# Weights' sign by a parametric ReLU, high parts of w_out on VectorE, and the second tile turned by VectorE and DMA

## The chip, the cores and the metric

One NeuronCore of a Trainium2 chip. The metric is device time in microseconds, the median of several executions. TensorE (PE) multiplies, VectorE (DVE) and ScalarE (ACT) work element by element, GpSimd (POOL) does little here, and SyncE (SP) issues nearly all DMAs. Each engine takes its own list of instructions in order, and semaphores between the lists make one engine wait for another.

## The reference

Chunked attention (chunks of 64 tokens, 8 heads of 64) and behind it a feed-forward block with a piecewise quadratic activation. All inputs arrive in double precision.

```python
scores = scale * np.matmul(q_c, k_c.transpose(0, 1, 2, 4, 3))
attn = np.exp(scores - np.max(scores, axis=-1, keepdims=True))
attn = attn / (np.sum(attn, axis=-1, keepdims=True) + 1e-09)
out = np.matmul(attn, v_c)
...
h = x @ w_in
g = np.where(h >= 1, h, np.where(h <= -1, 0.0, (h + 1) ** 2 / 4))
return g @ w_out
```

There are 4608 tokens; x has 512 columns, w_in is 512 x 2048, w_out 2048 x 512.

## The kernel before

**Tiles.** The 4608 tokens are nine tiles t of 512 tokens. A tile has four groups g of two heads; group (t, g) is worked on as one [128, 512] piece. The feed-forward block has 16 steps j of 128 hidden columns: `ffn_in(t, j)` is twelve 512-column products (four chunks kc of x, each with three products of high and low parts), and `ffn_out(t, j - 2)`, two steps behind, is twelve more. `ffn_in` needs the split x of all four groups: chunk kc comes from group kc. So tile 1 of the feed-forward block can't go past its first three chunks until group (1, 3) of the attention is done.

**Attention of a group.** `attn_turn` turns q and k so that heads lie along partitions; `scores_of` multiplies (L420); `attn_softmax` takes the maximum (L474), on tile 1 eight exponentials that also sum (L483), the reciprocal and the scaling of e (L506); `attn_turn_back` turns e into aT; `values_of` multiplies aT with v (L441); `attn_split` writes the high part xh (ACT, L545) and the low part xl (DVE, L546). From the second tile on, the values of one group and the scores of the next stand together on PE (`attn_products`), and both use the bank pair `ps_a`. There is one buffer for each of qT, kT and x (in the attention's sense: the turned e), and two for e, aT and v.

**Two ways to turn.** Tiles below `FLIPPED` (here tiles 0 and 1) turn q, k and e by four PE transposes each (`flip`, L376) into a PSUM bank, which ACT evicts (L401, L529). Later tiles load q and k in blocks of 32 (`load_blocks`, 128-byte rows, four DMAs each), turn them by a DVE 32 x 32 stream transpose (L392), and turn e by a DVE transpose (L533) and eight DMAs on SP that put the blocks into place (`move`, L522).

**Weights.** All 32 weight chunks, 512 KB of doubles each, are loaded once (L249, L256) and made into a high and a low single-precision part by `prepare(w, j)` while tile 0 computes. A double is read as two 32-bit words. ACT scales the upper word, read as a float (L271); DVE shifts it left by three (L274); ACT scales the lower word (L277); DVE adds it (L281) and puts the sign bit in (L286); ACT rounds to the high part (L296); DVE subtracts for the low part (L300). Each step j of tile 0 prepares two chunks.

**The order.** Nothing is scheduled at run time. The kernel records each piece of work with an engine, a cost and what it reads and writes; `Plan.emit` then plays this through with its own clock and emits the instructions of each engine in the order of that play: of the pieces that are ready on a free engine, the one recorded first. A DMA's landing is put behind all DMAs planned before it:

```python
if moving:
    end = moved = max(end, moved) + moving
for m in users[n]:
    other = parts[m][0]
    delay = lag + (0.0 if other == e == "pe" else self.DELAY[e])
    ready[m] = max(ready[m], end + delay)
```

A weight load has `moving` 1.9, a blocked q or k load 2.2, the eight DMAs of `move` 0.4 and a cost of 4.8 on SP. So a changed cost, or another way to turn, moves pieces on every engine. At the start, where PE has nothing to do, dummy products (`warm`, L734) fill in.

Of the kernel before, what the change touches and what calls it, by code (L numbers as in the profile page):

```python
# [9 lines left out]
F32 = mybir.dt.float32  # L10
F32R = mybir.dt.float32r
AF = mybir.ActivationFunctionType
ALU = mybir.AluOpType
# [4 lines left out]
class Plan:  # L18
# [15 lines left out]
    def add(  # L34
        self, engine, cost, emit, reads=(), writes=(), lag=0.0, columns=0, port=False, moving=0.0
    ):
        n = len(self.parts)
        needs = {self.writer[k] for k in (*reads, *writes) if k in self.writer}
        for k in writes:
            needs.update(self.readers.pop(k, ()))  # L40
            self.writer[k] = n
        for k in reads:
            self.readers.setdefault(k, []).append(n)
        needs.discard(n)
        for k in writes:
            self.written.setdefault(k, []).append(n)
        self.parts.append((engine, cost, emit, needs, lag, columns, port, moving))
        return n
# [92 lines left out]
def kernel(  # L141
# [15 lines left out]
    nc = tc.nc  # L157
# [16 lines left out]
    SCALE = 1.0 / float(D) ** 0.5  # L174
    ALL = NTILE * NP

    FLIPPED = 2
    EARLY = 2

    BATCH = (0, 1, 2, 3, None, 4, 5, 6, 7)  # L180
# [35 lines left out]
    weight = {}  # L216

    def place(kind, w, j, shape, dtype):
        return sb.tile(shape, dtype, name=f"{kind}_{w}{j}", tag=f"{w}{j}")

    first = {}
    for w, j, names in (
# [5 lines left out]
        both = place("first", w, j, [P, 2, T], F32)  # L228
# [3 lines left out]
    def room(name, bufs, t, g):  # L232
        if t == 0 and (name, g) in first:
            return first[name, g]
        return bufs[(t * NP + g) % len(bufs)]

    plan = Plan()
    count = {"tmp": 0}

    def turn_of(name, bufs):  # L240
        count[name] += 1
        return bufs[count[name] % len(bufs)]
# [17 lines left out]
    def prepare(w, j):  # L260

        both = (f"{w}{j}_0", f"{w}{j}_1")
        ykey, yf = turn_of("tmp", tmp_bufs)
        y = yf.bitcast(U32)

        def half(n):
            return words[w, j].rearrange("p (n two) -> p n two", two=2)[:, :, n]

        plan.add("act", 0.52, lambda: nc.scalar.activation(  # L271
            out=yf, in_=half(1).bitcast(F32), func=AF.Copy, scale=2.0 ** -112
        ), both, (ykey,))
        plan.add("dve", 0.34, lambda: nc.vector.tensor_scalar(  # L274
            out=y, in0=y, scalar1=3, scalar2=None, op0=ALU.logical_shift_left
        ), (), (ykey,), port=True)
        plan.add("act", 0.52, lambda: nc.scalar.activation(  # L277
            out=half(0), in_=half(0), func=AF.Copy, scale=2.0 ** -29
        ), (), both)

        plan.add("dve", 0.6, lambda: nc.vector.tensor_tensor(  # L281
            out=y, in0=y, in1=half(0), op=ALU.add
        ), both, (ykey,), port=True)

        def sign():
            nc.vector.scalar_tensor_tensor(  # L286
                out=y, in0=half(1), scalar=0x80000000, in1=y,
                op0=ALU.bitwise_and, op1=ALU.bitwise_or,
            )
            words.pop((w, j))  # L290

        plan.add("dve", 0.6, sign, both, (ykey,), port=True)

        def high():
            weight[w, j] = place("parts", w, j, [P, 2, T], F32R)
            nc.scalar.copy(out=weight[w, j][:, 0, :], in_=yf)  # L296

        def low():
            hi, lo = (weight[w, j][:, n, :] for n in range(2))
            nc.vector.tensor_tensor(out=lo, in0=yf, in1=hi.bitcast(F32), op=ALU.subtract)  # L300

        plan.add("act", 0.52, high, (ykey,), both)
        plan.add("dve", 0.6, low, (ykey, both[0]), (both[1],), port=True)


# [50 lines left out]
    def load_heads(t, g, which="qkv"):  # L356
        for n, src, bufs in (("q", q, q_bufs), ("k", k, k_bufs), ("v", v, v_bufs)):
            if n not in which:
                continue
            key, dst = room(n, bufs, t, g)  # L360
            load = load_values if n == "v" else load_rows if t < FLIPPED else load_blocks
            parts = 4 if load == load_blocks else 2
# [22 lines left out]
    def attn_turn(t, g):  # L385
        for n, (name, bufs, src_bufs, dst_bufs) in enumerate(
# [3 lines left out]
            dkey, dst = room(bufs, dst_bufs, t, g)  # L390
            if t >= FLIPPED:
                plan.add("dve", 0.6, lambda src=src, dst=dst: nc.vector.transpose(  # L392
# [34 lines left out]
    def values_of(t, g):  # L427
# [6 lines left out]
        def emit():  # L434
            for n in range(CT // 2):
                for h in range(2):
                    at = (2 * n + h) * C if t < FLIPPED else h * HALF + n * C
                    of = h * HALF + n * C
# [24 lines left out]
    def attn_softmax(t, g):  # L463
# [4 lines left out]
        e3 = e.rearrange("p (n k) -> p n k", k=C)  # L468
        e4 = e.rearrange("p (n h k) -> p h n k" if t < FLIPPED else "p (h n k) -> p h n k", h=2, k=C)
        mx4 = mx.rearrange("p (h n) x -> p h n x", h=2)  # L470
        sm4 = sm.rearrange("p (n h) x -> p h n x" if t < FLIPPED else "p (h n) x -> p h n x", h=2)
        sc = pair[:, :, :HALF].rearrange("p h (n k) -> p h n k", k=C)
# [37 lines left out]
    def attn_turn_back(t, g):  # L510
# [14 lines left out]

        if t < FLIPPED:
            pkey, ps = o_banks[1] if t == 0 else a_banks[0]
# [148 lines left out]
    load_more(6)  # L676
    load_heads(1, 1)
    prepare("wi", 0)
    prepare("wi", 1)
    prepare("wi", 2)  # L680

    LAG = 2
# [91 lines left out]
```

## Time and profile before

| | |
|---|---|
| timed runs | 865.99, 866.38, 867.03 us; median 866.38 |
| span of the profiled execution | 864.3 us, 14919 instructions |
| PE | busy 858.2 us (99%) |
| DVE, ACT | busy 443.8 us (51%), 382.6 us (44%) |
| DMA | 62.86 MB, mean 73 GB/s; 235920 of 250965 packets under 512 B |

The page gives the span of one profiled execution; of that execution's own time beyond the span it shows nothing, so the timed runs stand beside it. Durations of one row can overlap with the next on the same engine; where that matters, the distance between starts is used. A row of the timeline reads: start, length (us), engine, line, operation, output<-input, shapes, count. TensorE's granted clock is 1.00 in all windows of the profile.

### The profile page before, as it was taken

Reading aid. Unit: us, or ns where it says so; the run is one execution under the profiler, and the core shown is the slowest. Engines: PE = TensorE matmul, PEld = TensorE weight load, DVE = VectorE, ACT = ScalarE, POOL = GpSimd, SP = SyncE. Lnnn points to the kernel's source line nnn. Section 1 sums busy time; section 2 is a strip of 40 time slices with the busy share of each in tenths; the row PEclk is TensorE's granted clock in tenths of the full one; section 3 lists DMA queues with packets and bytes.
Section 4 is the critical chain, followed back from the end, with each engine's and each line's share of the span. In section 5 each row is a group of like instructions: output and inputs, shape, how many; then the busy total and the mean of one; then the engine's idle time right before and its main releaser. Section 6 shows DMA issues by size and latency. Waiting matters only on the chain.

```text
span 864.3 us, 14919 instructions
## 1 busy us (share of the span) xinstructions
PE 858.2 (99%) x5958; PEld 706.7 (82%) x5958; DVE 443.8 (51%) x762; ACT 382.6 (44%) x704; POOL 4.9 (1%) x10
## 2 busy tenths in 40 slices
PE   9999999999999999999999999999999999999998
PEld 8788788888888888888888888888888888888886
DVE  5999986444544444444544454445444444423222
ACT  5999965333433343333333343334333333333332
POOL 1000000000000000000000000000000000000000
PEclk9999999999999999999999999999999999999999
DMA  9997235322322232223322242223222310001001
GB/s 209 324 350 190 38 69 121 58 50 47 82 46 47 44 88 52 51 38 57 90 50 50 50 95 52 47 46 94 48 39 46 79 33 14 13 1 50 1 0 49
DMA packets 250965, 62.86 MB, mean 73 GB/s; under 512 B 235920, under 2 KB 244368, under 8 KB 250896
## 3 DMA queue, kind: packets, MB, share of 16 engines
q1 hardware_dynamic: 248640, 61.25, 31.7%
q8 instruction: 47, 0.77, 0.4%
q10 hardware_dynamic: 2256, 0.66, 0.4%
q14 instruction: 22, 0.18, 0.1%
HBM read 45.09 MB, written 9.44 MB: 63 GB/s over the span
## 4 chain that ended last, share of the span: by engine, by line
PE 91%; ACT 5%; DVE 2%; issue 1%; DMA 0%; POOL 0%; DVEq 0%; POOLq 0%; ACTq 0%
PE ps_h L562 42%; PE ps_o L597 41%; PE ps_a L441 2%; PE ps_a L420 2%; PE ps_h L734 1%; PE ps_a L597 1%; ACT tmp L271 1%; PE ps_o L376 1%; ACT r L572 1%; ACT words_wi L277 1%; ACT r L569 1%; ACT e L483 1%; ACT parts_wi L296 0%; DVE tmp L281 0%; ACT words_wo L277 0%
## 5 line engine op out<-in xcount | busy, mean ns | idle before, releaser
L562 PE MATMUL ps_h<-xh,parts_wi 128*128 128x512 f32 x1144 | 382.0, 393 | 0.0
L597 PE MATMUL ps_o<-parts_wo,gh 128*128 128x512 f32 x1120 | 346.1, 390 | 0.6 <-DVE parts_wo L300 0.4
L562 PEld LDWEIGHTS ps_h<-xh,parts_wi 128*128 128x128 f32 x1144 | 214.7, 188 | 46.2 <-DVE r L573 0.2
L597 PEld LDWEIGHTS ps_o<-parts_wo,gh 128*128 128x128 f32 x1120 | 209.6, 188 | 44.8 <-DVE parts_wo L300 0.7
L573 DVE SCALAR_TENSOR_TENSOR r<-ps_h,r 128x512 f32<-128x512 f32 x143 | 97.3, 681 | 259.1 <-ACT r L572 259.0
L562 PE MATMUL ps_h<-xl,parts_wi 128*128 128x512 f32 x572 | 222.9, 390 | 0.0
L597 PE MATMUL ps_o<-parts_wo,gl 128*128 128x512 f32 x560 | 218.0, 389 | 0.4 <-DVE gl L583 0.4
L569 ACT ACTIVATE r<-ps_h 128x512 f32<-128x512 f32 x143 | 86.1, 602 | 279.0 <-PE ps_h L562 279.0
L582 ACT CAST gh<-r 128x512 fp32r<-128x512 f32 x144 | 90.3, 627 | 147.8 <-PE ps_o L597 96.3
L583 DVE TENSOR_TENSOR gl<-r,gh 128x512 fp32r<-128x512 f32 x144 | 98.3, 682 | 107.1 <-ACT gh L582 106.9
L562 PEld LDWEIGHTS ps_h<-xl,parts_wi 128*128 128x128 f32 x572 | 107.4, 188 | 21.2
L597 PEld LDWEIGHTS ps_o<-parts_wo,gl 128*128 128x128 f32 x560 | 105.1, 188 | 22.7 <-DVE gl L583 0.8
L572 ACT ACTIVATE r<-r 128x512 f32<-128x512 f32 x144 | 91.6, 636 | 3.3
L474 DVE TENSOR_REDUCE mx<-ps_a 128x8 f32<-128x512 f32 x34 | 23.4, 688 | 27.0 <-ACT xh L545 18.0
L545 ACT CAST xh<-ps_a 128x512 fp32r<-128x512 f32 x34 | 20.0, 588 | 19.7 <-PE ps_a L420 19.2
L441 PEld LDWEIGHTS ps_a<-aT,v_sb 64*64 64x64 f32 x1056 | 18.4, 134 | 11.5 <-issue 10.8
L499 DVE TENSOR_REDUCE sm<-e 128x8 f32<-128x512 f32 x30 | 20.5, 685 | 10.7 <-ACT e L493 10.6
L441 PE MATMUL ps_a<-aT,v_sb 64*64 64x64 f32 x1056 | 22.9, 224 | 0.0
L546 DVE TENSOR_TENSOR xl<-ps_a,xh 128x512 fp32r<-128x512 f32 x34 | 22.4, 658 | 0.2 <-ACT xh L545 0.2
L506 DVE TENSOR_TENSOR e<-e,sm 128x512 f32<-128x512 f32 x32 | 21.8, 682 | 0.0
L420 PE MATMUL ps_a<-kT,qT 64*64 64x64 f32 x1056 | 21.4, 218 | 0.0
L533 DVE STREAM_TRANSPOSE x<-e 128x512 f32<-128x512 f32 x28 | 19.9, 711 | 0.9
(95 smaller groups left out, 422.8 us busy)
## 6 DMA issues: line engine op xcount, KB each, us to landing
words_wi<-in_moe_w_in_dram SPq DMA_DIRECT2D x16, 512.0 KB, 7.0
words_wo<-in_moe_w_out_dram SPq DMA_DIRECT2D x16, 512.0 KB, 7.1
out_dram<-tmp SPq DMA_DIRECT2D x31, 256.0 KB, 2.5
v_sb<-in_v_dram SPq DMA_DIRECT2D x60, 128.0 KB, 3.0
aT<-x SPq DMA_DIRECT2D x224, 32.0 KB, 1.9
q_sb<-in_q_dram SPq DMA_DIRECT2D x96, 64.0 KB, 2.2
k_sb<-in_k_dram SPq DMA_DIRECT2D x96, 64.0 KB, 2.3
q_sb<-in_q_dram SPq DMA_DIRECT2D x12, 128.0 KB, 6.6
```

The source lines that it names most:

```text
L420: nc.tensor.matmul(out=pair[i * C:(i + 1) * C, half, n * C:(n + 1) * C], lhsT=qT[rows, at], rhs=kT[rows, at], start=True, stop=True,)
L441: nc.tensor.matmul(out=pair[h * C:(h + 1) * C, half, HALF + n * C:HALF + (n + 1) * C], lhsT=v_sb[rows, of:of + C], rhs=aT[rows, at:at + C] ...
L474: plan.add("dve", 0.6, lambda: nc.vector.tensor_reduce(out=mx4, in_=sc, axis=AX.X, op=ALU.max), pkeys, (mkey,))
L506: plan.add("pool" if on_pool else "dve", 1.05 if on_pool else 0.6, lambda: eng.tensor_tensor(out=e3, in0=e3, in1=sm.broadcast_to([P, G, C] ...
L546: plan.add("dve", 0.6, lambda: nc.vector.tensor_tensor(out=of_tokens(xl), in0=ps, in1=of_tokens(xh.bitcast(F32)), op=ALU.subtract), (*pkey ...
L562: nc.tensor.matmul(out=ps, lhsT=weight["wi", j][:, half, kc * P:(kc + 1) * P], rhs=x, start=(kc == 0 and i == 0), stop=(kc == KC - 1 and i ...
L569: plan.add("act", 0.48, lambda: nc.scalar.activation(out=r, in_=ps, func=AF.Relu, bias=0.5, scale=0.5), (pkey,), (rkey,))
L572: plan.add("act", 0.52, lambda: nc.scalar.square(out=r, in_=r), (), (rkey,))
L573: plan.add("dve", 0.6, lambda: nc.vector.scalar_tensor_tensor(out=r, in0=ps, scalar=1.0, in1=r, op0=ALU.max, op1=ALU.min), (pkey,), (rkey,))
L582: plan.add("act", 0.52, lambda: nc.scalar.copy(out=gh, in_=r), (rkey,), (ghkey,))
L583: plan.add("dve", 0.6, lambda: nc.vector.tensor_tensor(out=gl, in0=r, in1=gh.bitcast(F32), op=ALU.subtract), (rkey, ghkey), (glkey,), port ...
L597: nc.tensor.matmul(out=acc, lhsT=x[:, cols], rhs=weight["wo", j][:, half, :], start=(j == 0 and i == 0), stop=(j == NF - 1 and i == 2),)
```

## The change

Three things. The sign of a weight is no longer put in by DVE: ACT scales the upper word with a parametric ReLU whose slope for negative inputs is 2^32, which adds 32 to the exponent of a negative number, so that the shift by three moves that bit to the sign's place. The high part of a w_out chunk is copied by DVE, that of a w_in chunk by ACT as before. And `FLIPPED` goes from 2 to 1, so tile 1 is loaded and turned as the later tiles are. Some costs of the plan change as well.

```diff
-    FLIPPED = 2
+    FLIPPED = 1
...
-        plan.add("act", 0.52, lambda: nc.scalar.activation(
-            out=yf, in_=half(1).bitcast(F32), func=AF.Copy, scale=2.0 ** -112
+        plan.add("act", 0.56, lambda: nc.scalar.activation(
+            out=yf, in_=half(1).bitcast(F32), func=AF.Prelu, scale=2.0 ** -112, alpha=2.0 ** 32
         ), both, (ykey,))
-        plan.add("dve", 0.34, lambda: nc.vector.tensor_scalar(
+        plan.add("dve", 0.38, lambda: nc.vector.tensor_scalar(
             out=y, in0=y, scalar1=3, scalar2=None, op0=ALU.logical_shift_left
         ), (), (ykey,), port=True)
-        plan.add("act", 0.52, lambda: nc.scalar.activation(
+        plan.add("act", 0.56, lambda: nc.scalar.activation(
             out=half(0), in_=half(0), func=AF.Copy, scale=2.0 ** -29
         ), (), both)
-        plan.add("dve", 0.6, lambda: nc.vector.tensor_tensor(
-            out=y, in0=y, in1=half(0), op=ALU.add
-        ), both, (ykey,), port=True)
-
-        def sign():
-            nc.vector.scalar_tensor_tensor(
-                out=y, in0=half(1), scalar=0x80000000, in1=y,
-                op0=ALU.bitwise_and, op1=ALU.bitwise_or,
-            )
+        def add():
+            nc.vector.tensor_tensor(out=y, in0=y, in1=half(0), op=ALU.add)
             words.pop((w, j))
-        plan.add("dve", 0.6, sign, both, (ykey,), port=True)
+        plan.add("dve", 0.6, add, both, (ykey,), port=True)
         def high():
             weight[w, j] = place("parts", w, j, [P, 2, T], F32R)
-            nc.scalar.copy(out=weight[w, j][:, 0, :], in_=yf)
+            hi = weight[w, j][:, 0, :]
+            if w == "wo":
+                nc.vector.tensor_copy(out=hi, in_=yf)
+            else:
+                nc.scalar.copy(out=hi, in_=yf)
...
-        plan.add("act", 0.52, high, (ykey,), both)
+        if w == "wo":
+            plan.add("dve", 0.38, high, (ykey,), both, port=True)
+        else:
+            plan.add("act", 0.52, high, (ykey,), both)
```

The emitted order changes on every engine. Three places follow; L numbers behind `prepare` differ by a few between the two kernels (L282 is the add, L291 the copy on DVE, L293 the one on ACT, L297 the subtraction of the changed kernel).

**PE, end of tile 0 and start of tile 1.** xh_1_ and xl_1_ rows are the first products of tile 1's feed-forward block; L441 and L420 are the values of one group and the scores of the next. Before, the last two groups of tile 1, with the flip of e between them:

```order
L376 MATMUL ps_a<-ident,e_77 128x128 x4
L562 MATMUL ps_h_116<-xh_1_90,parts_wi_287 128x512
L562 MATMUL ps_h_116<-xl_1_98,parts_wi_287 128x512
L562 MATMUL ps_h_116<-xh_1_90,parts_wi_287 128x512
L597 MATMUL ps_o_113<-parts_wo_1383,gh_103 128x512 x2
L597 MATMUL ps_o_113<-parts_wo_1383,gl_105 128x512
L597 MATMUL ps_o_114<-parts_wo_1383,gh_103 128x512 x2
L597 MATMUL ps_o_114<-parts_wo_1383,gl_105 128x512
L441 MATMUL ps_a<-aT_79,v_sb_73 64x64 x16
L420 MATMUL ps_a<-kT_75,qT_74 64x64 x16
L597 MATMUL ps_o_111<-parts_wo_1383,gh_103 128x512 x2
```

In the changed kernel, the values of (1, 2) and of (1, 3):

```order
L597 MATMUL ps_o_111<-parts_wo_1304,gl_106 128x512
L441 MATMUL ps_a<-aT_78,v_sb_72 64x64 x16
L420 MATMUL ps_a<-kT_75,qT_74 64x64 x16
L562 MATMUL ps_h_116<-xh_1_90,parts_wi_277 128x512
L562 MATMUL ps_h_116<-xl_1_98,parts_wi_277 128x512
L562 MATMUL ps_h_116<-xh_1_90,parts_wi_277 128x512
L562 MATMUL ps_h_115<-xh_1_90,parts_wi_415 128x512
L562 MATMUL ps_h_115<-xl_1_98,parts_wi_415 128x512
L562 MATMUL ps_h_115<-xh_1_90,parts_wi_415 128x512
L441 MATMUL ps_a<-aT_79,v_sb_73 64x64 x16
L420 MATMUL ps_a<-kT_75,qT_74 64x64 x16
```

Counted over the list, 48 products stood between these two L441 before, and six stand there now, the third chunk of the first two steps of tile 1. The first L441 of tile 1 moved from behind 129 products to behind 270, and from the one behind 504 products on, PE's list is the same in both kernels.

**SP, the last weight loads.** q_sb_68 and k_sb_70 are q and k of group (1, 2). Before:

```order
L249 DMA words_wi_609<-in_moe_w_in_dram 128x4x256
L317 DMA q_sb_68<-in_q_dram 64x8x64 x2
L317 DMA k_sb_70<-in_k_dram 64x8x64 x2
L256 DMA words_wo_655<-in_moe_w_out_dram 128x1024
L256 DMA words_wo_671<-in_moe_w_out_dram 128x1024
```

Now:

```order
L249 DMA words_wi_672<-in_moe_w_in_dram 128x4x256
L331 DMA q_sb_68<-in_q_dram 32x16x32 x4
L331 DMA k_sb_70<-in_k_dram 32x16x32 x4
L522 DMA aT_78<-x_80 32x8x32 x8
L256 DMA words_wo_782<-in_moe_w_out_dram 128x1024
```

The eight DMAs that bring back the turned e of group (1, 0) stand behind 29 of the 32 weight loads; q and k are issued in four pieces each.

**DVE, from the scores of (1, 3) to its turned e.** In the changed kernel, behind the last weight chunk:

```order
L474 TENSOR_REDUCE mx_82<-ps_a 128x8
L392 STREAM_TRANSPOSE qT_74<-q_sb_68 128x512
L546 TENSOR_TENSOR xl_1_98<-ps_a,xh_1_90 128x2x4x64
L479 TENSOR_SCALAR mx_82<-mx_82 128x8
L392 STREAM_TRANSPOSE kT_75<-k_sb_70 128x512
L500 TENSOR_SCALAR sm_84<-sm_84 128x8
L501 RECIPROCAL sm_84<-sm_84 128x8
L506 TENSOR_TENSOR e_77<-e_77,sm_84 128x512
L533 STREAM_TRANSPOSE x_80<-e_77 128x512
```

No row of the weights or of the feed-forward block stands among them any more; the transpose at the end is new for tile 1.

## The prediction

> **What bounds the kernel now.** I read the page's busy shares first, then PE's own waits, then busy time by windows, and last the rows of the places that the change touches.
>
> ```profile
> PE 858.2 (99%) x5958; PEld 706.7 (82%) x5958; DVE 443.8 (51%) x762; ACT 382.6 (44%) x704; POOL 4.9 (1%) x10
> ...
> PE ps_h L734 <- POOL ident masks.py:199: 1.4, 1, 1.4
> PE ps_o L597 <- DVE parts_wo L300: 0.4, 1, 0.4
> PE ps_o L597 <- DVE gl L583: 0.4, 1, 0.4
> PE ps_o L597 <- ACT parts_wo L296: 0.2, 1, 0.2
> ```
>
> PE is busy for 99% of the span, and the list of PE's waits has four entries: 1.4 us at the very start and 1.0 us in all after it. So before the change no chain of other engines is late anywhere; the time is PE's list of instructions. That holds although the stages differ:
>
> ```profile
> 50.00:60.00 10.00, 10.00 (x53) 7.95 (x53) 9.88 (x18) 10.00 (x21) 0.00 (x0) 1.00 1.05 395
> 75.00:80.00 5.00, 5.00 (x24) 4.14 (x23) 5.00 (x10) 5.00 (x10) 0.00 (x0) 1.00 0.95 180
> 80.00:90.00 10.00, 10.00 (x90) 8.07 (x92) 10.00 (x19) 9.57 (x19) 0.00 (x0) 1.00 0.32 53
> 140.00:160.00 20.00, 20.00 (x207) 16.53 (x207) 11.22 (x20) 7.37 (x12) 0.00 (x0) 1.00 0.45 99
> ```
>
> Columns after the length: PE, PEld, DVE, ACT, POOL, then PE's clock (1.00), DMA share, GB/s. At 50 us, where weights are prepared, DVE, ACT and DMA are as full as PE; DMA is free from 80 us, DVE and ACT from about 125. From 140 us PE alone is full. Its unit there:
>
> ```profile
> 156.29 0.62 PE ps_a L441 x32
> 156.91 0.47 PE ps_a L420 x32
> 157.38 2.95 PE ps_h L562 x12
> 160.33 2.72 PE ps_o L597 x12
> ...
> 179.37 0.62 PE ps_a L441 x32
> ```
>
> Twelve 512-column products take 2.72 us, 0.2267 each. By the order 96 of them lie between these two value steps, which start 23.08 apart, so a pair of values and scores costs 23.08 - 96 x 0.2267 = 1.32 us.
>
> **What leaves PE: the flips of tile 1.** Twelve (q, k, e of four groups) go.
>
> ```profile
> 31.77 0.39 PE L562 MATMUL ps_h<-xh,parts_wi 128*128 128x512 f32 x1
> 32.00 0.60 PE L376 MATMUL ps_a<-ident,q_sb 128*128 128x128 f32 x4
> 32.36 0.48 PE L562 MATMUL ps_o<-xh,parts_wi 128*128 128x512 f32 x1
> 32.67 0.40 PE L562 MATMUL ps_o<-xl,parts_wi 128*128 128x512 f32 x1
> ```
>
> Starts show the cost: the next product begins 0.36 after the flip, and the one behind it 0.31 later where 0.23 is usual. 0.36 + 0.08 = 0.44 each, 5.3 us in all. If nothing else moved, that would be the gain.
>
> **The start.**
>
> ```profile
> 26.17 1.06 PE L734 MATMUL ps_o<-ident 128*128 128x128 f32 x8
> 27.16 0.69 PE L441 MATMUL ps_o<-first_wi,first_wo 64*64 64x64 f32 x32
> ```
>
> PE fills time with dummy products ahead of the fourth group's values at 27.16. Without the sign the second w_in chunk is ready sooner, and the order now puts six more real products ahead of those values: 6 x 0.2267 = 1.4 us. I take 1.0 (bounds 0 and 1.4): the same list on DVE must first finish the copies and splits of the groups behind. The 24 products that were done at 32.00 are then done at 31.0.
>
> **VectorE and ScalarE between.**
>
> ```profile
> 33.54 0.68 DVE L573 SCALAR_TENSOR_TENSOR r<-ps_h,r 128x512 f32<-128x512 f32 x1
> ...
> 42.52 0.76 DVE L274 TENSOR_SCALAR tmp<-tmp 128x512 uint32<-128x512 uint32 x2
> 43.20 0.68 DVE L281 CUSTOM_DVE_ANT_0 tmp<-words_wo,tmp 128x1024 uint16<-128x1024 uint16 x1
> 43.80 0.68 DVE L281 CUSTOM_DVE_ANT_0 tmp<-words_wi,tmp 128x1024 uint16<-128x1024 uint16 x1
> 44.40 0.68 DVE L286 SCALAR_TENSOR_TENSOR tmp<-words_wo,tmp 128x512 uint32<-128x512 uint32 x1
> ...
> 57.73 0.76 ACT L296 CAST parts_wo<-tmp 128x512 fp32r<-128x512 f32 x1
> 58.23 0.74 ACT L401 COPY kT<-ps_a 128x512 f32<-128x512 f32 x1
> ```
>
> By starts a shift takes 0.34 (two in 0.68) and any two-input operation 0.60. DVE loses 32 signs (19.2 us) and gains 12 turns of tile 1 (a row below has 0.70, so 0.62 with the same overlap of 0.08; 7.4) and 16 high parts of w_out. The trace has no such copy; it lies between 0.34 (the shift: one input in SBUF, four bytes) and 0.60. I take 0.34, the row that it is nearest to in form: 5.4 us. In sum DVE gets 6.4 us less. ACT loses 16 copies and 12 evictions of about 0.50 by starts, 14 us. A Prelu isn't in the trace; I cost it as the Copy that it replaces, and even at 0.4 more for each of 32 ACT would be no fuller than before, so either end is hidden. In the new order DVE has, from its first gate (the first row above, 33.5) up to the maximum of group (1,1), 21 shifts, 11 copies, 4 turns and 69 operations of 0.60: 7.1 + 3.7 + 2.5 + 41.4 and 0.4 of small ones, 55 us, so it gets there at 88.5. That matters below.
>
> The page "VectorE: DVE Perf Modes" of the Trainium skill, section "Mode 2×_2P", says that a one-input operation between SBUF tensors uses both read ports and runs at double rate even in fp32. By it a copy takes what the shift's row has and the sum is 878.1; at single rate it would be 881.0. No run here shows the copy yet.
>
> **What is added: a longer way from scores to values.** A tile's transposed weights come back by DVE and eight DMAs in place of a flip and an eviction. Tile 1 and tile 2 side by side:
>
> ```profile
> 112.17 0.65 PE L420 MATMUL ps_a<-kT,qT 64*64 64x64 f32 x32
> 119.31 0.68 DVE L506 TENSOR_TENSOR e<-e,sm 128x512 f32<-128x512 f32 x1
> 121.72 0.60 PE L376 MATMUL ps_a<-ident,e 128*128 128x128 f32 x4
> 124.34 0.69 PE L441 MATMUL ps_a<-aT,v_sb 64*64 64x64 f32 x32
> ...
> 124.86 0.65 PE L420 MATMUL ps_a<-kT,qT 64*64 64x64 f32 x32
> 131.74 0.70 DVE L533 STREAM_TRANSPOSE x<-e 128x512 f32<-128x512 f32 x1
> 132.51 5.29 SPq L522 DMA_DIRECT2D aT<-x  x8
> 139.94 0.69 PE L441 MATMUL ps_a<-aT,v_sb 64*64 64x64 f32 x32
> ...
> 156.22 0.69 PE L441 MATMUL ps_a<-aT,v_sb 64*64 64x64 f32 x32
> ...
> aT<-x SPq DMA_DIRECT2D x224, 32.0 KB, 1.9
> ```
>
> On tile 2 the transpose ends 7.6 us after the scores start, the last of eight issues starts 4.7 later (5.29 less one issue of 0.6), and lands after 1.9: 14.3 us, at most the 15.1 to the row of the values. On tile 1, with busier engines, the normalized weights are ready at 7.8 and the transpose would end at 8.5. While PE has other products this costs nothing. The order says how many it has. PE takes its list in order, and these are the products between value steps (first groups of tile 1, then tile 2):
>
> before: (1,0) after 129, (1,1) 246, (1,2) 327, (1,3) 375, (2,0) 438, (2,1) 504;
> now: 270, 342, 396, 402, 432, 504.
>
> The first value step stands 141 products later, since on SP the new DMAs of (1,0) follow the weight loads; the other three are then crowded to the end of tile 0. Between (1,2) and (1,3) stand six products, 1.4 us, under a chain of 14. From 504 on PE's list is the same in both, so I compare there: before it is the row at 156.22.
>
> Step by step. (1,0): 31.0 + 246 x 0.2267 + 0.7 for the scores of (1,0) = **87.5**; DVE's 88.5 for the next maximum fits (scores end at 88.6). (1,1): scores 88.0, DVE has two weight chunks between, some 2.6 us, so the transpose ends at 98.2 and the DMAs land at 104.8; PE needs 1.32 + 72 x 0.2267 = 17.6 and comes at 105.1: no wait. (1,2): scores 105.6, PE comes at 105.1 + 1.32 + 54 x 0.2267 = 118.7; the chain takes 15.1 with the last gates ahead of it on ACT, 120.7: **2.0 of wait**. (1,3): scores 121.2; only six products, which themselves wait for the split of (1,2); chain 14.3 on idle engines: 135.5, **about 13 us with 1.4 of work in them**. (2,0): scores 136.0; 30 products, 6.8 us, that wait for the split of (1,3) and for the first bank, some 5 us, so that PE comes at about 148; chain 14.3: 150.3, **2 of wait**. (2,1): 150.3 + 1.32 + 72 x 0.2267 = **167.9**. That is 11.7 us later than 156.22, flips and start already counted.
>
> **DMA: does (1,0) land in time?**
>
> ```profile
> 63.63 4.37 SPq L317 DMA_DIRECT2D k_sb<-in_k_dram  x2
> ...
> q1 hardware_dynamic: 248640, 61.25, 31.7%
> words_wo<-in_moe_w_out_dram SPq DMA_DIRECT2D x16, 512.0 KB, 7.1
> ```
>
> The new DMAs stand behind this k load, whose issue ends at 68.0. q and k of tile 1 come in twice as many packets; a packet takes 0.317 x 16 x 864.3 / 248640 = 17.6 ns on average, so 1024 more cost 0 to 1.1 us per transfer, 0 to 6.8 for the six ahead. I take half. 68.0 + 3.4 + 5.3 + 7.1 = 83.8, at worst 87.2, under PE's 87.5. Hidden; past it each us is one us later at (1,0) and after.
>
> **Sum.** The profiled span is 864.3; the median of the timed runs, 866.4, lies 2.1 above, which I take for what surrounds it. 864.3 + 11.7 + 2.1 = **878.1 us**, 1.4% slower.
>
> **Rivals.** *The turn hides, and the flips are won.* For: the flips do cost PE 5.3, and DVE and ACT are relieved. Against: six products under a chain of 14.3. A shorter chain takes three times its gain off the total for the first 2 us, at (1,2), (1,3) and (2,0), and after that once, at (1,3) alone: the 11.7 are gone at a chain of 14.3 - 2 - 5.7 = 6.6, that is if the weights were back as soon as the transpose ends (7.6), with the DMAs at nothing. Past that point flips, start and the 1.0 of old waits are the gain: 866.4 - 7.3 = 859. Chance 0.03, and 0.02 that it stops near no change, 866. *The copies on DVE run at 0.60*: 11 of them before the maximum of (1,1) put DVE 2.9 later there, with nothing to spare: 881.0; 0.10. *The landing of (1,0) is late*: if the small packets cost PE's whole margin and 6 us more, 884; 0.06. My forecast: 0.79.
>
> **Range.** Chains of 13.5 instead of 14.3 take off 2.4 and a start gain of 1.4 takes 0.4; busier engines (15.1 on all three, or 0.8 more each) add 2.4, no gain at the start 1.0, the slow copies 2.9: 874.0 to 884.0. Faster by over 0.2% (about what a measurement of this kernel can tell from no change) 0.03, within it 0.02, slower 0.95.
>
> **What would show it.** L376 with 12 groups fewer; no DVE sign rows; the copy's row at 0.34 between starts; PE waits that name the DMAs aT<-x at the value steps of tile 1, the longest near 9 to 10 us just before 136, and PE at some 5 or 6 tenths in the two slices from 108 to 151 us; from there on units of 23.08 as now. If PE shows no such waits, the reading of the order is wrong; if they stand at (1,0), it is the DMA queue; if DVE is busy throughout them, the copies.

## The result and the profile after

The changed kernel takes **880.38 us** (median of 4 runs, 879.92 to 881.10) beside 866.52 before: a ratio of 1.0162, interval 1.0149 to 1.0174. It is slower by 13.9 us, where 878.1 (874.0 to 884.0) had been forecast. The profiled span is 878.1 us, 13.8 longer than before.

From the page of the changed kernel: the first row of busy times, and of the 40 slices those of PE and of its granted clock.

```profile
PE 859.0 (98%) x5910; PEld 706.2 (80%) x5910; DVE 441.9 (50%) x758; ACT 369.4 (42%) x676; POOL 4.9 (1%) x10
...
PE   9999966999999999999999999999999999999998
...
PEclk9999986999999999999999999999999999999999
```

PE has 48 instructions fewer (12 flips of four), and the hole is in two slices, from about 110 to 154 us; everything behind them looks as before. PE's busy time is nevertheless the same as before, 859.0 against 858.2: at a lower clock products last longer, so busy time hides part of the hole. The list of PE's waits names it:

```profile
PE ps_a L441 <- DMA aT<-x: 9.7, 3, 6.0
PE ps_h L562 <- ACT xh L545: 2.8, 2, 1.4
...
PE ps_h L562 <- DVE r L573: 1.3, 1, 1.3
```

A row gives PE's instruction, what it waited for, the sum in us, the number of waits and the longest. There are three waits before value steps, for the eight DMAs that bring aT. Behind them stand short waits of the first products of tile 1: two for the split of the group that has just come (xh), and one for VectorE's r. The timeline has the places. These are the value steps of (1,0) to (2,1), a row or two each; the number in brackets is PE's wait ahead of the row:

```profile
88.96 0.69 PE L441 MATMUL ps_a<-aT,v_sb 64*64 64x64 f32 x32
...
106.60 0.69 PE L441 MATMUL ps_a<-aT,v_sb 64*64 64x64 f32 x32
...
120.16 0.32 PE L441 MATMUL ps_a<-aT,v_sb 64*64 64x64 f32 x2
122.01 0.63 PE L441 MATMUL ps_a<-aT,v_sb 64*64 64x64 f32 x27 [1.53 <-DMA aT<-x]
...
133.85 0.45 PE L441 MATMUL ps_a<-aT,v_sb 64*64 64x64 f32 x2 [6.05 <-DMA aT<-x]
136.40 1.02 PE L441 MATMUL ps_a<-aT,v_sb 64*64 64x64 f32 x27 [2.11 <-DMA aT<-x]
...
152.05 0.95 PE L441 MATMUL ps_a<-aT,v_sb 64*64 64x64 f32 x29
...
170.04 0.69 PE L441 MATMUL ps_a<-aT,v_sb 64*64 64x64 f32 x32
```

The last row, (2,1), stood at 156.22 before. 170.04 - 156.22 = 13.8 is the whole difference of the two spans: all of the loss lies ahead of this row, and nothing behind it. A step is split in two where its first products find their blocks landed and the others don't.

The chain of one group, from the scores of (1,3) to its values, on four engines:

```profile
122.49 0.68 PE L420 MATMUL ps_a<-kT,qT 64*64 64x64 f32 x31
...
123.22 0.69 DVE L474 TENSOR_REDUCE mx<-ps_a 128x8 f32<-128x512 f32 x1 [1.64 <-PE ps_a L420]
...
128.31 0.69 DVE L506 TENSOR_TENSOR e<-e,sm 128x512 f32<-128x512 f32 x1
129.04 0.71 DVE L533 STREAM_TRANSPOSE x<-e 128x512 f32<-128x512 f32 x1
...
129.79 5.17 SPq L522 DMA_DIRECT2D aT<-x  x8
```

From these scores to the values at 136.4 it is 13.9 us (that the loss has the same size is chance). About half is softmax on nearly empty engines, and half is the turn: the transpose, 5.2 us of issues on SP, and 1.4 more until the values start. No engine is full in it; PE has six products for the whole time.

### The profile page after: what moved, and what is told of

Its sections match the earlier page's. It is cut to its first block, busy times and chain, and to the rows that moved or that the text cites. A ratio compares the mean times of both kernels' runs of the same rounds, so it can differ in the third digit from the quotient of the medians.

```text
span 878.1 us, 14874 instructions
## 1 busy us (share of the span) xinstructions
PE 859.0 (98%) x5910; PEld 706.2 (80%) x5910; DVE 441.9 (50%) x758; ACT 369.4 (42%) x676; POOL 4.9 (1%) x10
## 4 chain that ended last, share of the span: by engine, by line
PE 89%; SPq 1%; DVE 1%; DMA 1%; ACT 1%; issue 0%; DVEq 0%
PE ps_h L562 43%; PE ps_o L597 41%; PE ps_a L441 2%; PE ps_a L420 2%; PE ps_a L597 1%; SPq L522 1%; SPq L331 0%; DMA aT<-x 0%; DMA k_sb<-in_k_dram 0%; ACT e L483 0%; DMA out_dram<-tmp 0%; DVE r L573 0%; DVE mx L474 0%; DVE gl L583 0%; DVE qT L392 0%
## 5 line engine op out<-in xcount | busy, mean ns | idle before, releaser
L597 PE MATMUL ps_o<-parts_wo,gh 128*128 128x512 f32 x1120 | 344.9, 389 | 0.0
L597 PEld LDWEIGHTS ps_o<-parts_wo,gh 128*128 128x128 f32 x1120 | 210.3, 188 | 43.7
L597 PE MATMUL ps_o<-parts_wo,gl 128*128 128x512 f32 x560 | 218.0, 389 | 0.0
L597 PEld LDWEIGHTS ps_o<-parts_wo,gl 128*128 128x128 f32 x560 | 105.1, 188 | 22.2 <-DVE gl L583 0.5
L441 PEld LDWEIGHTS ps_a<-aT,v_sb 64*64 64x64 f32 x1056 | 19.5, 137 | 21.7 <-issue 21.6
L441 PE MATMUL ps_a<-aT,v_sb 64*64 64x64 f32 x1056 | 24.4, 227 | 9.7 <-DMA aT<-x 9.7
L533 DVE STREAM_TRANSPOSE x<-e 128x512 f32<-128x512 f32 x32 | 22.7, 711 | 1.0
L392 DVE STREAM_TRANSPOSE qT<-q_sb 128x512 f32<-128x512 f32 x32 | 22.5, 702 | 0.0
L392 DVE STREAM_TRANSPOSE kT<-k_sb 128x512 f32<-128x512 f32 x32 | 22.4, 700 | 0.0
```

The source lines that it names most:

```text
L441: nc.tensor.matmul(out=pair[h * C:(h + 1) * C, half, HALF + n * C:HALF + (n + 1) * C], lhsT=v_sb[rows, of:of + C], rhs=aT[rows, at:at + C] ...
L533: plan.add("dve", 0.6, lambda: nc.vector.transpose(out=x, in_=e), (ekey,), (xkey,))
L597: nc.tensor.matmul(out=acc, lhsT=x[:, cols], rhs=weight["wo", j][:, half, :], start=(j == 0 and i == 0), stop=(j == NF - 1 and i == 2),)
```

## The experiments

Value steps stand in PE's list where the planner's own play puts them, so the table has, for each version, the products ahead of the value steps, and what was measured. "aT" is the sum of PE's waits on these DMAs, (1,0) and (2,1) the starts of these steps in the profiled run.

| kernel | products ahead of (1,0), (1,1), (1,2), (1,3), (2,0) | (1,0) | aT | (2,1) | time | ratio to before, 95% |
|---|---|---|---|---|---|---|
| before | 129, 246, 327, 375, 438 | 59.9 | 0 | 156.2 | 866.5 | |
| changed | 270, 342, 396, 402, 432 | 89.0 | 9.7 | 170.0 | 880.4 | 1.0149 to 1.0174 |
| e1 weights' edits alone | 123, 252, 324, 372, 435 | 58.0 | 0 | 154.4 | 864.3 | 0.9968 to 0.9987 |
| e2 turn alone | 282, 345, 396, 402, 432 | 95.7 | 11.6 | 179.8 | 889.8 | 1.0252 to 1.0286 |
| e3 copies back on ACT | 273, 348, 396, 402, 435 | 88.7 | 10.5 | 169.5 | 880.0 | 1.0142 to 1.0172 |
| e4 DMAs on two queues | 270, 339, 396, 402, 435 | 90.4 | 12.5 | 175.0 | 885.0 | 1.0193 to 1.0224 |
| e5 dummy products in waits | as changed, but 438 at (2,0) | 89.9 | 2.7 | 171.2 | 879.8 | 1.0135 to 1.0167 |
| e6 DMAs on ScalarE | 111, 249, 315, 390, 444 | 57.2 | 0 | 166.3 | 875.2 | 1.0089 to 1.0119 |
| e7 DMAs on GpSimd | 132, 267, 360, 402, 435 | 57.9 | 6.1 | 162.8 | 874.9 | 1.0084 to 1.0117 |
| e8 GpSimd, no lag | 126, 267, 324, 378, 441 | 57.8 | 2.9 | 154.8 | 865.4 | 0.9981 to 1.0000 |
| e9 GpSimd, lag kept | 129, 270, 336, 396, 450 | 57.0 | 3.9 | 162.2 | 871.5 | 1.0045 to 1.0078 |
| e10 GpSimd, 3.6 us | 126, 267, 327, 384, 450 | 58.5 | 1.6 | 156.5 | 864.0 | 0.9964 to 0.9984 |
| e11 Prelu alone | 138, 252, 327, 372, 435 | 61.9 | 0 | 154.9 | 864.1 | 0.9961 to 0.9981 |

(2,1) stands behind 504 products except in e6 (510), e8 (507), e9 and e10 (516); a product is 0.2267 us.

**e1, the weights' edits without the turn.** On the changed kernel:

```diff
-    FLIPPED = 1
+    FLIPPED = 2
```

> The second tile is turned by TensorE again; the Prelu and the copies of the high parts of w_out on VectorE stay. Theory (the whole loss comes with the turn of the second tile): no wait of PE before L441 names a DMA, the value step of (2,0) starts at 155 to 156.5 as before, time 865 to 867 (0.4 us from the start at most). Rival (the Prelu and the copies have a part in it, because VectorE is fuller when the second tile's attention needs it): 869 or more.

864.27, 0.7 below the range, and no wait on a DMA. (The step that stood at 156.2 before is (2,1), not (2,0) as the expectation has it; here it starts at 154.4.) There is no loss without the turn; the weights' edits by themselves gain 2.1 us, more than the 0.4 that the expectation allowed.

**e2, the turn without the weights' edits.** On the kernel before:

```diff
-    FLIPPED = 2
+    FLIPPED = 1
```

> The kernel before with the second tile's turn changed and nothing else: the sign stays a fourth pass on VectorE and the copies stay on ScalarE. Theory: the turn alone brings the loss, 879 to 884, with PE waits on DMA aT<-x between 115 and 155 of 8 to 14 us in all; a little later than the changed kernel because VectorE has 32 passes more. Rival (the weights' conversion carries 3 us or more of the 14): 877 or less.

889.82: almost 6 us above the range. The turn alone costs 23 us, and the changed kernel, with the weights' edits on top, only 14. So the two parts are not independent: the edits gain 2 alone and 9.4 beside the turn. Two views show where. First, from the list of PE's waits of this run:

```profile
PE ps_o L597 <- DVE parts_wo L300: 2.6, 3, 1.3
```

and then 90 to 125 us by windows, of this run and of the changed kernel (length, then PE, PEld, DVE, ACT, POOL busy, clock, DMA share, GB/s):

```profile
90.00:125.00 35.00, 33.13 (x260) 25.97 (x259) 33.91 (x65) 26.62 (x71) 0.00 (x0) 1.00 0.30 54
```

```profile
90.00:125.00 35.00, 32.06 (x264) 25.94 (x255) 26.43 (x52) 18.39 (x56) 0.00 (x0) 1.00 0.48 98
```

With the sign as a pass of its own VectorE is busy for 33.91 of these 35 us (26.43 in the changed kernel), PE waits for weights at L597, and the first value step comes at 95.68 instead of 88.96, 6.7 later, of which 2.7 are twelve more products ahead of it. At (2,1), 179.82, it is 9.8: the other 3.1 come on the way to (1,3). The turn's DVE work and the weights' DVE work meet in the same stretch.

**e3, the copies of w_out back on ScalarE.** On the changed kernel, in `high`:

```diff
-            if w == "wo":
-                nc.vector.tensor_copy(out=hi, in_=yf)
-            else:
-                nc.scalar.copy(out=hi, in_=yf)
+            nc.scalar.copy(out=hi, in_=yf)
...
-        if w == "wo":
-            plan.add("dve", 0.38, high, (ykey,), both, port=True)
-        else:
-            plan.add("act", 0.52, high, (ykey,), both)
+        plan.add("act", 0.52, high, (ykey,), both)
```

> The changed kernel with the high parts of w_out copied by ScalarE as before (16 copies of 0.34 us leave VectorE, 16 of about 0.72 us go to ScalarE). Theory (the chain from scores to values of one group bounds, and neither engine's load is in it): 879 to 881.5, the same waits. Rival (VectorE's load lengthens that chain): 877 or less.

880.03, nearly the same waits: the place of the copies doesn't matter here. This run differs from e2 by the Prelu alone, with the planner's costs and the order that go with it; so the 9.4 beside the turn come with the Prelu in place of the sign's pass, and not with the copies.

**e4, the DMAs of a turn on two queues.**

```diff
...
-            plan.add("sp", 4.8, move, (xkey,), (akey,), lag=1.7, moving=0.4)
+            if t > 1:
+                plan.add("sp", 4.8, move, (xkey,), (akey,), lag=1.7, moving=0.4)
+                return
+            plan.add("sp", 2.4, lambda: move((0,)), (xkey,), (akey,), lag=1.7, moving=0.4)
+            plan.add("act", 2.4, lambda: move((1,), nc.scalar), (xkey,), (akey + "b",),
+                     lag=1.7, moving=0.4)
```

> The changed kernel, the eight DMAs that finish a turn of the second tile issued in two halves, four by SP and four by ScalarE; the planner is told 2.4 us for each half instead of 4.8. Theory (the loss is the length of the chain scores to values, of which the issue of eight DMAs is 5.2 us): the chain becomes 2 to 2.5 us shorter, PE waits before (1,2) and (1,3) fall from 9.7 to about 6 us, (2,0) starts at 147 to 149 instead of 152.05, time 874.5 to 877. Rival 1 (the landing of the last DMA is set by the DMA engines, not by SP's issue): no change, 879.5 or more. Rival 2 (ScalarE's issue delays its own work as much): 879.5 or more, with ScalarE named in the waits.

884.97: slower, and neither rival names why. SP's rows ahead of (1,1), then ScalarE's and SP's half for (1,3) and the values:

```profile
94.22 10.15 SPq L331 DMA_DIRECT2D q_sb<-in_q_dram  x4
...
106.59 2.55 SPq L520 DMA_DIRECT2D aT<-x  x4
...
135.50 2.58 ACTq L520 DMA_DIRECT2D aT<-x  x4
...
137.53 2.80 SPq L520 DMA_DIRECT2D aT<-x  x4
...
141.76 1.13 PE L441 MATMUL ps_a<-aT,v_sb 64*64 64x64 f32 x32 [9.29 <-DMA aT<-x]
```

For (1,3), SP's half starts 2 us behind ScalarE's though it needs nothing else. SP's list of waits says for what: a landing of the same DMAs (L520). Its loads of q and k (L331), which have nothing to do with aT, wait for such landings too:

```profile
SPq L331 <- DMA aT<-x: 14.5, 4, 8.3
...
SPq L520 <- DMA aT<-x: 5.5, 2, 3.4
```

So it is not the buffer that the two halves share. In the trace the DMAs of SP and of ScalarE signal through the same eight semaphores, and in these places a DMA is held until the one that used its semaphore last has landed. SP's half for (1,3) starts at 137.53, when the first of ScalarE's four has landed (137.46), not the last (139.39). Worse is the load of q at 94.22: it stands for 8.3 us until a DMA of ScalarE's half for (1,1) lands at 102.8, so SP's own half of (1,1) starts only at 106.59, and PE waits 3.2 us for it at 110.6. Most of what this run loses beside the changed kernel arises there.

The chain of (1,3) stayed at 13.6 us (scores at 128.1, values at 141.8). The run added waits where it was meant to take one away, so it says nothing about a shorter chain.

**e5, PE kept busy in the waits.** 26 dummy products (6 ahead of the values of (1,2), 20 ahead of (1,3)) into the half of `ps_a` whose scores have been read:

```diff
...
+    left = {(1, 2): 6, (1, 3): 20}
...
+                warm(a_pair[:, 0, :])()
...
     plan.emit(("pe", 0.215, 512, (
+        *((refill(at), read[at], valued[at]) for at in left),
```

> The changed kernel with 26 dummy products on a free half of ps_a (6 ahead of the value step of (1,2), 20 ahead of that of (1,3)), so that PE is not idle in its longest waits. Theory (the lower clock of 125 to 149 us costs nothing, since the DMAs of the turn of (2,0) land at 152 either way): the granted clock in 140 to 150 us is back above 0.8, and the time stays within 1 us, 879.4 to 881.4; the time saved by PE turns up as a wait before (2,0). Rival (the clock is part of the loss: some 18 products at 0.43 instead of 0.227 us are 3.6 us): 876 to 878.

879.83, the same as without. The expectation was met in the time but not in the clock: the windows of this run (clock behind POOL's column) have

```profile
130.00:140.00 10.00, 7.73 (x104) 7.37 (x104) 2.08 (x4) 0.00 (x0) 0.00 (x0) 0.82 0.30 48
140.00:150.00 10.00, 7.89 (x17) 5.49 (x18) 7.48 (x14) 4.89 (x8) 0.00 (x0) 0.52 0.53 92
```

against 0.50 and 0.56 in the changed kernel: the dummies held it up to 140 and not beyond. The waits on DMA fell to 2.7 us because dummies stand in them; (2,1) came 1.2 us later in the profiled run, not sooner.

**e6 and e7, the DMAs of tile 1 on another queue.** On SP they stand behind the weight loads, and the planner moreover puts their landing behind every planned landing of a weight. Here an engine of its own issues them, and the landing follows the issue:

```diff
...
-            plan.add("sp", 4.8, move, (xkey,), (akey,), lag=1.7, moving=0.4)
+            if t > 1:
+                plan.add("sp", 4.8, move, (xkey,), (akey,), lag=1.7, moving=0.4)
+                return
+            plan.add("act", 4.8, lambda: move(queue=nc.scalar), (xkey,), (akey,),
+                     lag=1.7, moving=0.0)
```

In e7 `"pool", 8.0` and `nc.gpsimd` stand in place of `"act", 4.8` and `nc.scalar`.

> The changed kernel with the second tile's turns back issued by ScalarE instead of SP, where they don't stand behind the loads of the weights, and the planner told so (it lets the landing follow the issue). Theory (the loss is the late start of (1,0) in a chain of four groups: each us earlier gives a us back, up to the 13.8 that stand before (2,1)): the value step of (1,0) moves from 88.96 to 56 to 68 us, no PE wait on DMA aT<-x above 1.5 us, (2,1) at 152 to 158, time 859 to 867. Rival 1 (ScalarE's 5 us of issuing at about 50 us makes the weights late there): (1,0) early but PE waits for parts_wi or parts_wo at 50 to 80 us, 868 to 876. Rival 2 (the step of one group, some 14 to 18 us, is what bounds, wherever the chain begins): 876 or more.

> The same on GpSimd's queue, an engine with 5 us of work in all (the planner is told 8 us for eight DMAs, about which nothing was measured here). Theory: as in the run with ScalarE's queue, without its cost on ScalarE, 859 to 868 if GpSimd issues eight DMAs within some 8 us; with a slower issue PE waits on DMA aT<-x at (1,1) to (1,3) as now, up to 880. Rival (chain bounds wherever it begins): 876 or more.

875.21 and 874.85. (1,0) starts 31 us earlier in both, but only 5 to 6 us of time come back, for different reasons. With ScalarE the time is that of rival 1. PE's waits of e6 name no DMA at all; the two longest are for r and gh of the feed-forward block:

```profile
PE ps_h L564 <- DVE r L575: 2.8, 1, 2.8
PE ps_o L599 <- ACT gh L584: 2.8, 1, 2.8
```

The one for gh, at 55.6 us, comes right behind an issue of ScalarE; the one for r, at 140.0, has its like in the changed kernel (1.3) and in e9 (2.05). The waits for weights that the rival named are 2.2 us in sum. ScalarE stands still while it issues, here in the middle of preparing weights:

```profile
49.05 5.32 ACTq L520 DMA_DIRECT2D aT<-x  x8
54.41 0.62 ACT L293 CAST parts_wi<-tmp 128x512 fp32r<-128x512 f32 x1 [5.07 <-DMA aT<-x]
```

How much of the loss of e6 this makes is not shown, since SP is held up here as in e4: its loads wait 37 us in all for landings of these DMAs. In e7 the DMAs on GpSimd's queue have eight semaphores of their own, and no such wait is in SP's list.

With GpSimd it is the crowding again, though the first step is back in its place. The planner, told 8 us, wrote 360, 402 and 435 for (1,2) to (2,0): 42 products, 9.5 us, stand under the chain of (1,3). The DMAs of that group, and its values:

```profile
121.83 4.60 POOL L520 DMA_DIRECT2D aT<-x  x8 [13.62 <-issue]
```

```profile
126.47 0.30 PE L441 MATMUL ps_a<-aT,v_sb 64*64 64x64 f32 x2 [2.08 <-DMA aT<-x]
129.34 1.02 PE L441 MATMUL ps_a<-aT,v_sb 64*64 64x64 f32 x27 [2.57 <-DMA aT<-x]
```

So an early start is not enough, and the theory as written for these runs, "each us earlier gives a us back", was too simple.

**e8, e9 and e10, the spacing.** GpSimd's queue throughout, only the planner's numbers differ: e9 tells it 3.0 us for the eight issues instead of the 8.0 of e7, e8 also drops the lag of 2.2 us that it put ahead of the multiplication by the reciprocals, and e10 is e8 with 3.6. On e7, the edit that makes e8:

```diff
     def late(t, lag):
-        return lag if t == 1 else 0.0
+        return 0.0
...
-            plan.add("pool", 8.0, lambda: move(queue=nc.gpsimd), (xkey,), (akey,),
+            plan.add("pool", 3.0, lambda: move(queue=nc.gpsimd), (xkey,), (akey,),
                      lag=1.7, moving=0.0)
```

> As the run on GpSimd's queue, where eight DMAs took 4.6 to 5.0 us to issue and (1,1) and (1,2) stood late only because of the order that the planner wrote (267, 360, 402, 435 products ahead of the value steps of (1,1) to (2,0)): here the planner is told 3.0 us and no lag of 2.2 us before the multiplication of the second tile, and writes 267, 324, 378, 441, as far apart as before the change (246, 327, 375, 438). Theory (only the crowding of the value steps costs time: a group's chain of 14 to 16.5 us is hidden where 54 to 66 products, 12.3 to 15 us, and the value step stand between two of them): waits on DMA aT<-x of 0 to 4 us, (2,1) at 150.5 to 155, time 859 to 864, faster than both kernels. Rival (a chain of four groups at 15.7 to 16.7 us each cannot be hidden): (2,0) at 145 or later, 868 or more.

> The same with the lag of 2.2 us kept: the value steps stand behind 270, 336, 396, 450 and 516 products, later and closer at (1,3). Theory: between the two runs on GpSimd's queue, waits of 2 to 6 us at (1,3), time 861 to 869. Rival: 870 or more.

> As the run on GpSimd's queue without the lag, the planner told 3.6 us instead of 3.0: the value steps stand behind 126, 267, 327, 384, 450 products, where it were 267, 324, 378, 441. Theory (what is left of the waits there, 1.2 us ahead of (1,2) and 1.35 ahead of (1,3), goes when the two stand 3 and 6 products, 0.7 and 1.4 us, later): waits on DMA aT<-x under 1.5 us in all, 863 to 865. Rival (each step later moves the next chain as much later, and a wait returns at the next): 865 to 868.

865.42, 871.47 and 863.98. Nothing of the work differs between the changed kernel and these three but who issues 32 DMAs and in what order the lists were written, and with 57, 54, 63 (e8) or 60, 57, 66 (e10) products between the value steps of (1,1) to (2,0), 12.2 to 15 us, the loss is gone in e8 and e10. e7 and e8 differ in nothing but these two numbers, and so in the order, by 9.4 us. e8 missed its range by 1.4 us; e10 met its own, with 1.6 us of waits on DMA where under 1.5 had been expected.

e9 missed by 2.5 and came out where its rival stood, with spacings of 66, 60 and 54 that are hardly worse. Its waits on DMA are 3.9 us, as forecast; what it loses beyond that is to be seen, in its largest part, in four us behind one wait. The rows are PE's timeline of e9, and one window of e9 and of e8 (length, PE busy, clock, DMA share, GB/s):

```profile
134.73 0.80 PE L564 MATMUL ps_h<-xh,parts_wi 128*128 128x512 f32 x1 [2.05 <-DVE r L575]
135.32 0.63 PE L564 MATMUL ps_h<-xl,parts_wi 128*128 128x512 f32 x1
```

```profile
134.00:138.00 4.00, 3.27 (x8) 0.57 0.80 166
```

```profile
134.00:138.00 4.00, 4.00 (x20) 1.00 0.33 62
```

PE waits 2.05 us for VectorE, and then its clock is at half: eight products begin in a window in which e8 has 20. Here PE is itself the bound, so the 0.2 us by which each of them is longer are lost too, some 1.6 in all. The same follows the wait before (1,0), where the clock is 0.55 from 59 to 62 us (1.00 in e8).

e10's busy row, and the first of the six entries in its list of PE's waits, which add up to 5.2 us:

```profile
PE 852.8 (99%) x5910; PEld 701.9 (81%) x5910; DVE 440.7 (51%) x758; ACT 369.3 (43%) x676; POOL 23.8 (3%) x42
```

```profile
PE ps_a L441 <- DMA aT<-x: 1.6, 3, 0.6
```

**e11, the Prelu alone.** The changed kernel with the tile turned by TensorE (as e1) and the copies on ScalarE (as e3).

> The kernel before with the Prelu alone: the second tile turned by TensorE, the copies of w_out on ScalarE. Theory (what the weights' edits gain, 2.1 us in the run with both, is VectorE's fourth pass taken away): 864 to 865.5. Rival (the copies on VectorE bring it, because ScalarE is then free earlier): 866 or more.

864.10, with the copies (e1) 864.27: the Prelu brings all that the weights' edits gain. Its page against that of e10:

```profile
PE 857.2 (99%) x5956; PEld 706.6 (82%) x5956; DVE 428.5 (50%) x730; ACT 381.4 (44%) x704; POOL 4.9 (1%) x10
```

In e10 PE has 4.4 us less to do, mostly the flips, and yet the two spans differ by 0.6 (862.4 and 863.0) and the times by nothing: its waits add up to 5.2 us, the two of e11 (the 1.4 of the start and 0.8 at a value step of tile 0) to 2.2. The cheaper way to turn is paid back in waits even at its best. e10 is faster than both kernels of this study, but so is e11, with a far smaller change.

## Why the prediction was right

**The direction and the mechanism were right, step by step.** The value steps of tile 1, crowded behind 396, 402 and 432 products, wait for their own chains; the waits name the DMAs, the longest ends at 133.85 and goes on, two products later, to 136.40 (6.05 and 2.11 us, where one of 9 to 10 had been forecast), and PE's units are as before from (2,1) on. Forecast and measured starts:

| | (1,0) | (1,1) | (1,2) | (1,3) | (2,0) | (2,1) |
|---|---|---|---|---|---|---|
| forecast | 87.5 | 105.1 | 120.7 | 135.5 | 150.3 | 167.9 |
| measured | 88.96 | 106.60 | 122.01 | 136.40 | 152.05 | 170.04 |

e8 and e10 show the cause: beside e7 they change the spacing alone, and the loss goes with the crowding. That the position of (1,0) behind the weight loads crowds the steps is shown by e6, where (1,1) to (2,0) stand 54 to 75 products apart once it is moved; that it is not all, by e7, where the planner's 8.0 us crowd them again.

**The start was mis-sized.** The prediction took 1.0 us of gain there. The first product row that ends a count of 24 is this:

```profile
31.36 0.62 PE L562 MATMUL ps_h<-xh,parts_wi 128*128 128x512 f32 x2
```

The first of the two is the 24th, done where the second starts, at about 31.6: a gain of 0.4, inside the bounds of 0 to 1.4. Another 0.9 on the way to (1,0) is short gaps on PE that I had taken as none (the products at 34.08 and 34.49 start 0.41 apart); with it (1,0) is 1.5 late, and that carries over to the steps behind it.

**The chain of (2,0) was mis-sized.** 14.8 us of step were forecast and 15.65 came (136.40 to 152.05). Its rows:

```profile
137.23 1.16 PE L420 MATMUL ps_a<-kT,qT 64*64 64x64 f32 x31
...
144.19 0.70 DVE L533 STREAM_TRANSPOSE x<-e 128x512 f32<-128x512 f32 x1
...
144.92 6.03 SPq L522 DMA_DIRECT2D aT<-x  x8
```

It is 0.83 us instead of 0.52 from values to scores, at half the clock, and 6.03 of issue instead of 5.29; the 7.7 between scores and turned e are as forecast. The steps to (1,2) and (1,3), 15.4 and 14.4, were 0.6 shorter in sum than forecast and that to (2,1) 0.4 longer, so that 1.5 + 0.85 - 0.6 + 0.4 make the 2.1 us by which (2,1) is late, nearly all of the 2.3 between 878.1 and 880.4.

**The wait at (2,0) did not come.** The prediction had PE there at about 148 and 2 us of wait. PE ran its products at half clock instead, without a gap from 144.33 to 152.05, and came just as the weights did: by the row above the last issue begins at about 150.3, and 1.9 later, at 152.2, it has landed. The step was bound by the chain, as forecast, so the sum didn't suffer; that PE wasn't later still is luck.

**The range.** Its bounds don't come out of the terms given for them: 878.1 - 2.4 - 0.4 is 875.3, not 874.0, and the terms upwards make 884.4, not 884.0. The measured 880.38 lies inside either way.

**The terms that held.** The next operation on VectorE begins 0.33 us after a copy, where 0.34 had been taken:

```profile
35.22 0.42 DVE L291 CAST parts_wo<-tmp 128x512 fp32r<-128x512 f32 x1
35.55 0.68 DVE L583 TENSOR_TENSOR gl<-r,gh 128x512 fp32r<-128x512 f32 x1
```

and a Prelu takes what the Copy took, by the line of it in the changed kernel and then in the kernel before (durations in ns: smallest, median, largest):

```profile
L271 ACT ACTIVATE tmp<-words_wi x16: 652/668/703, 10.9 to 87.1; 128x512 f32<-128x512 f32 x16
```

```profile
L271 ACT ACTIVATE tmp<-words_wi x16: 662/718/828, 11.1 to 100.2; 128x512 f32<-128x512 f32 x16
```

The rival of slow copies is out. The turn of (1,0) was issued from 76.77 on, later than worked out, and still landed at some 83.4 (last issue at 81.4, and 1.9 instead of the 7.1 taken), 5 us ahead of PE: the rival of the late landing is out too. The rival of a hidden turn is out for this order; for a better order it is what e10 shows, but without the 859 that it promised, since waits take the flips' 5 us back.

**What the prediction didn't see.** It took every product at 0.2267 us; that PE's clock falls behind a wait is told below. And it treated the weights' edits as a small gain beside the turn. e2 shows that they hold back another 9.4 us: VectorE's load up to about 124 us is on the path to the value steps of tile 1 as soon as the turn is VectorE's too. The prediction's list of VectorE's work up to the maximum of (1,1), "nothing to spare", had the fact in it. Alone, the Prelu shows in one place: of the 1.3 us between the profiled spans of before and e11 (864.3 and 863.0), 1.2 come between the 260th and the 280th product, at 93 to 99 us, where PE waited twice for the parts of w_out before (0.2 and 0.4 us) and waits no more. The rest of the 2.3 us between the times stays open.

## What to carry to other kernels

A latency is hidden by the work that stands between its start and its use in the list of the engine that would wait, so count that work at each place: six products under a chain of 14 us cost more than twelve flips saved, and 57 under the same chain cost almost nothing. When a step changes to another queue, ask what that queue already has ahead of it, what it shares with the others, and what the planner believes about it. Parts of a change that use the same engine in the same stretch have to be priced together: one of them was worth 2 us alone and 9 beside the other.

## What the runs showed that was not expected

**PE's clock falls in its waits.** TensorE's granted clock, 1.00 in every window before, by windows of the changed kernel (the clock stands behind POOL's column):

```profile
120.00:130.00 10.00, 4.74 (x72) 2.93 (x70) 5.16 (x10) 3.64 (x18) 0.00 (x0) 0.74 0.74 183
130.00:140.00 10.00, 2.63 (x65) 2.32 (x65) 1.53 (x3) 0.58 (x1) 0.00 (x0) 0.50 0.35 64
140.00:150.00 10.00, 8.69 (x22) 6.06 (x23) 6.52 (x12) 4.89 (x8) 0.00 (x0) 0.56 0.44 72
```

and single products there, the second pair after PE had run without a gap from 144.33 on:

```profile
144.93 0.63 PE L562 MATMUL ps_h<-xl,parts_wi 128*128 128x512 f32 x1
145.35 1.05 PE L562 MATMUL ps_h<-xh,parts_wi 128*128 128x512 f32 x2
...
148.76 0.39 PE L562 MATMUL ps_h<-xl,parts_wi 128*128 128x512 f32 x1
148.99 0.39 PE L562 MATMUL ps_h<-xh,parts_wi 128*128 128x512 f32 x1
```

0.42 us between starts, then 0.23 again, 4.4 us after the last gap. The Trainium skill, page "TensorE: Matmul & The Clock Gate", part 1, says that the gate halves the clock after an idle window of about 3.4 us and opens again after about as long a time of sustained work. For the opening these 4.4 us are near it. For the closing the traces differ: in e9 a wait of 2.05 us was enough, and in the changed kernel the clock is down from about 125 us on, behind waits of 1.53 and 1.41. In the changed kernel it seems to have cost little, because PE at half clock came to (2,0) at 152.05, and the weights only at about 152.2. That is argued from one step; e5 was to show it by itself and didn't hold the clock up beyond 140. In e9, where PE had work that nothing else held up, one wait of 2 us cost 1.6 more.

**GpSimd issues as fast as SP.** Eight DMAs took 4.6 to 5.0 us on GpSimd's queue (e7), 5.2 to 6.0 on SP's (changed kernel) and 5.3 on ScalarE's at 49 us (e6), where the engine's own work stood still meanwhile. They landed later, though: 3.0 us after the issue in the median in e7 and 2.4 in e10, where SP's took 1.9.

**Queues of SP and ScalarE wait for each other's landings**, whatever they fill, where their DMAs signal through the same semaphores: 8.3 us at most in e4, in a load of q. GpSimd's DMAs of e7 to e10 signal through others, and SP's lists of waits name them nowhere.
